# The last output DMA of a gated attention and GLU kernel in two parts, and one weight load in one piece

## The chip, the cores and the metric

The kernel runs on one core of a Trainium2 chip. The metric is device time in microseconds (us) of one execution; of several executions the median is given. A profile of one execution goes with it: its times are microseconds from the first instruction, and its span runs from the first to the last instruction. The engines are TensorE (PE; its weight loads are PEld), VectorE (DVE), ScalarE (ACT), GpSimd (POOL) and SyncE (SP). A `q` behind a name (SPq, ACTq) marks what the engine's sequencer does by itself: issuing DMAs, waiting for semaphores. Sixteen DMA engines move data between the chip's main memory and the core's own memory.

## The reference

One input `x` of 2048 rows and 512 columns (bf16) goes through a linear attention block and through a gated SwiGLU block, and a gate for each row mixes both:

```python
x = A_x
g = _sigmoid((x * gate_w).sum(-1, keepdims=True))
a = _A_ref(x, A_wqkv, A_wo)        # 32 heads of 16; phi(q), phi(k); kv and z summed over the rows
b = _B_ref(x, B_w1, B_w3, B_w2)    # (silu(x @ w1) * (x @ w3)) @ w2, 1376 hidden columns
return g * a + (1 - g) * b
```

The output has 2048 rows of 512 bf16 values, 2.10 MB in all.

## The kernel before, in words

All is unrolled into one straight program, and the order of every engine's instructions is the order in which the kernel's text gives them. Rows are taken in 16 tiles of 128 (`t`) or 4 blocks of 512 (`tb`).

- **Loads (lines 108 to 143).** Nearly all DMAs are issued by SP (`dq = nc.sync`), one after the other: the first rows `xN` (line 116), the projection weights `wqk` (113), 14 transposed loads of `x` into `xT` (110) with natural loads `xN` between them (128), the gate column and the remainder columns `wr` (130 to 134), then `w1` in one DMA and `w3` in two (the loop of lines 135 to 137), `wv` (138), `wo` (139) and `w2` (142, 143). ACT issues a single DMA, `touch` (line 120), 8 KB at the very start, whose data nothing reads.
- **Projections (lines 339 to 374).** `q` and `k` of each row tile by matmul (line 167), the function phi on ACT and DVE (lines 180 to 187), sums on POOL (199), and the products of `pk` and `xN` (line 215).
- **GLU (`glu_step`, lines 257 to 274).** For each of the 4 blocks and each of 10 column chunks of 128: four matmuls with `w1` (line 262), four with `w3` (line 268), silu on ACT, product on DVE into `hT`. The 96 remaining columns are done by `rem_step` (221 to 255). In the first block the small attention matrices (`kv_step` with `wv`, `m2_step` with `wo`) are made between the chunks.
- **Output (`out_step`, lines 408 to 444).** For each row tile: four matmuls give the attention part (line 414), ACT scales it by the gate into `aga` (419), eleven matmuls with `w2` give the GLU part (427), DVE combines both into `o` (431), and SP writes the rows of `o` to memory (444). For the last tile (`last`) the columns are computed in three strips, 256, 128 and 128 wide. The first strip is written by a DMA of its own; the second is not written by itself (lines 439 to 443), and the third one's DMA writes the last 256 columns, 128 rows of 512 B.

Each DMA carries a completion semaphore out of eight that are used in rotation over all DMAs of the program, SP's and ACT's together; a DMA from the ninth on first waits until the DMA eight places before it has landed. At the program's end SP waits for all completion semaphores, and a barrier over the five engines follows (its instructions bear the line of the launch, L493; L498 in the changed kernel, whose lines from 441 on stand five lower).

Of the kernel before, what the change touches and what calls it, by code (L numbers as in the profile page):

```python
# [16 lines left out]
def kernel(  # L17
# [17 lines left out]
    nc = tc.nc  # L35
    P = nc.NUM_PARTITIONS
# [5 lines left out]
    KC = D // P  # L42
# [15 lines left out]
    w1_r = B_w1.rearrange("(kc d) f -> d kc f", d=P)  # L58
    w3_r = B_w3.rearrange("(kc d) f -> d kc f", d=P)
# [16 lines left out]
        out=bmask[:], in_=bmask[:], pattern=[[-Dh, HPC], [0, Dh]], compare_op=ALU.is_ge,  # L76
# [3 lines left out]
        out=bmask[:], in_=bmask[:], pattern=[[Dh, HPC], [0, Dh]], compare_op=ALU.is_ge,  # L80
# [20 lines left out]
    w1 = consts.tile([P, KC, F0], BF16, name="w1")  # L101
    w3 = consts.tile([P, KC, F0], BF16, name="w3")
# [3 lines left out]
    dq = nc.sync  # L106
# [22 lines left out]
    with nc.allow_non_contiguous_dma(reason="gate column"):  # L129
        dq.dma_start(  # L130
            out=wr[:, :, 2 * FR : NR], in_=gate_w.rearrange("(kc d o) -> d kc o", d=P, o=1)
        )
    dq.dma_start(out=wr[:, :, 0:FR], in_=w1_r[:, :, F0:F])
    dq.dma_start(out=wr[:, :, FR : 2 * FR], in_=w3_r[:, :, F0:F])
    for w, w_r, cuts in ((w1, w1_r, (0, KC)), (w3, w3_r, (0, 2, KC))):
        for a, b in zip(cuts, cuts[1:]):
            dq.dma_start(out=w[:, a:b, :], in_=w_r[:, a:b, 0:F0])
    dq.dma_start(out=wv[:], in_=wqkv_r[:, :, 2 * D : 3 * D])
# [22 lines left out]
    def ab_tile():  # L161
        turn["ab"] += 1
        return bank[(turn["ab"] - 1) % 4]
# [244 lines left out]
    def out_step(tb, tt):  # L408
        t = tb * TPB + tt
        ts = slice(t * P, (t + 1) * P)  # L410
        tl = slice(tt * P, (tt + 1) * P)
        a_ps = ab_tile()
        for c in range(KC):
            nc.tensor.matmul(  # L414
                a_ps[:], lhsT=pqT[:, c, ts], rhs=M2[:, c, :],
                start=(c == 0), stop=(c == KC - 1),
            )
        aga = work.tile([P, D], FP32, tag="aga", name="aga")
        nc.scalar.activation(out=aga[:], in_=a_ps[:], func=ACT.Copy, scale=g_all[:, t : t + 1])  # L419
        o = work.tile([P, D], BF16, tag="o", bufs=3, name="o")  # L420
        last = t == NT - 1
        for lo, w in ((0, 2 * P), (2 * P, P), (3 * P, P)) if last else ((0, D),):
            cs = slice(lo, lo + w)
            b_ps = ab_tile()
            for fc in range(FC + 1):
                n = P if fc < FC else FR
                nc.tensor.matmul(  # L427
                    b_ps[:, 0:w], lhsT=hT[tb][:n, fc, tl], rhs=w2[:n, fc, cs],
                    start=(fc == 0), stop=(fc == FC),
                )  # L430
            nc.vector.scalar_tensor_tensor(  # L431
                out=o[:, cs], in0=b_ps[:, 0:w], scalar=omg_all[:, t : t + 1], in1=aga[:, cs],
                op0=ALU.mult, op1=ALU.add,
            )
            if t < 2:
                rows = out2d[0 : 2 * P, :].rearrange("(p j) d -> p j d", j=2)[:, t, :]
            else:
                rows = out2d[ts, :]
            if last and w == P:

                if lo + w < D:
                    continue
                cs = slice(2 * P, D)
            dq.dma_start(out=rows[:, cs], in_=o[:, cs])

    den_products(0)
    den_at = {0: 0, 1: 1, 3: 2, 6: 3}
    for tb in range(NTB):
        for fc in range(FC):
            glu_step(tb, fc)  # L450
            if tb == 0:
                if fc in den_at:
                    den_step(den_at[fc])
                if fc == 2:
                    kv_step()
                if fc == 4:
                    m2_step()
                if fc == 7:
                    rem_step(0)
        for tt in range(TPB):  # L460
            out_step(tb, tt)
            if tb + 1 < NTB:
                if tt == 0:
                    hT[tb + 1] = work.tile([P, FC + 1, TB], BF16, tag="hT", name="hT")
                if tt == 1:
                    rem_step(tb + 1)
                den_step((tb + 1) * TPB + tt)
# [30 lines left out]
```

## Time and profile before

| what | value |
|---|---|
| median of 3 runs | 179.43 us (179.19 to 179.78) |
| the profiled execution | 179.22 us |
| its span | 177.5 us |
| PE matmul busy | 173.9 us, 98% |
| DVE, ACT, POOL busy | 100.5, 62.3, 62.9 us |
| granted TensorE clock | 1.00 |
| bytes read and written in main memory | 8.43 and 2.10 MB |
| output DMAs | 15 of 128 KB (median 1.9 us to landing), 2 of 64 KB (1.5 us) |

The page's section 2 cuts the span into 40 slices of 4.4 us; each digit is the busy share of a slice in tenths. Section 4 follows the chain that ended last back from the last instruction. In rows of instructions, "x3: 351/351/484" is a count and the shortest, median and longest duration in ns; "DMA to landing" is counted from the start of the issue to the last of a DMA's completion marks. A DMA has up to 16 such marks, one from each DMA engine. The trace also holds a record of every DMA packet with its queue, start, duration and size.

### The profile page before, as it was taken

The page shows a single profiled execution, that of the slowest core. Times are in us where ns is not written, and L with a number is a line of the kernel's source. Part 1 is how long each engine was busy: PE and PEld are TensorE (multiplying, and loading weights), DVE is VectorE, ACT ScalarE, POOL GpSimd, SP SyncE. Part 2 cuts the span into 40 slices and gives each one's busy share as a digit, 9 for nine tenths or more (in the row PEclk, how much of TensorE's full clock was granted, in tenths as well). Part 3 has the DMA queues.
Part 4 walks back from the last instruction along what each step waited for, and adds up shares of the span by engine and source line. Part 5 has one row for each costly group of instructions (what it writes and reads, how often), then busy time and mean ns, then how long its engine had stood idle before and what let it go on. Part 6 is the DMA issues. An engine that isn't in the chain of part 4 may idle for free.

```text
span 177.5 us, 2504 instructions
## 1 busy us (share of the span) xinstructions
PE 173.9 (98%) x880; PEld 84.1 (47%) x880; DVE 100.5 (57%) x195; ACT 62.3 (35%) x113; POOL 62.9 (35%) x105
## 2 busy tenths in 40 slices
PE   8999999999999999999999999999999999999993
PEld 5444444444454464644444464444445444444453
DVE  1399788888899663575434166634325664433222
ACT  3354544444735441332342223142322223342130
POOL 5086656656577240446200044540004432000000
PEclk9999999999999999999999999999999999999999
DMA  5989869994002120233100013520000342000001
GB/s 174 269 202 216 163 106 264 406 381 142 4 0 59 30 47 16 59 82 96 30 0 4 0 40 80 90 63 0 0 0 30 89 92 59 0 0 0 30 33 59
DMA packets 28940, 15.15 MB, mean 85 GB/s; under 512 B 20896, under 2 KB 27264, under 8 KB 28928
## 3 DMA queue, kind: packets, MB, share of 16 engines
q1 hardware_dynamic: 28656, 14.98, 32.3%
q8 instruction: 7, 0.11, 0.3%
q14 instruction: 5, 0.04, 0.1%
q10 hardware_dynamic: 272, 0.01, 0.1%
HBM read 8.43 MB, written 2.10 MB: 59 GB/s over the span
## 4 chain that ended last, share of the span: by engine, by line
PE 98%; DVE 0%; issue 0%
PE bank L427 21%; PE bank L262 19%; PE bank L268 19%; PE bank L167 16%; PE bank L414 8%; PE bank L215 8%; PE bank L229 3%; PE bank L315 2%; PE bank L389 1%; PE bank L402 0%; PE bank L321 0%; DVE o L431 0%; PE bank L376 0%
## 5 line engine op out<-in xcount | busy, mean ns | idle before, releaser
L274 DVE TENSOR_TENSOR hT<-bank,sg 128x512 bf16<-128x512 f32 x40 | 27.2, 681 | 30.9 <-PE bank L268 30.9
L268 PE MATMUL bank<-xT,w 128*128 128x512 bf16 x160 | 41.1, 379 | 0.0
L262 PE MATMUL bank<-xT,w 128*128 128x512 bf16 x160 | 41.1, 379 | 0.0
L427 PE MATMUL bank<-w,hT 128*128 128x512 bf16 (+3 forms) x198 | 40.7, 355 | 0.0
L273 ACT ACTIVATE sg<-bank 128x512 bf16<-128x512 f32 x40 | 23.9, 597 | 46.9 <-PE bank L262 46.9
L296 POOL TENSOR_TENSOR pqs<-pq,rden 128x512 bf16<-128x512 bf16 x16 | 16.9, 1055 | 65.1 <-issue 60.0
L167 PE MATMUL bank<-wqk,xT 128*128 128x512 bf16 x128 | 30.6, 382 | 0.0
L431 DVE SCALAR_TENSOR_TENSOR o<-bank,omg_all,aga 128x512 bf16<-128x512 f32 (+2 forms) x18 | 12.5, 692 | 28.1 <-PE bank L427 28.0
L427 PEld LDWEIGHTS <-hT 128*128 128x128 bf16 (+1 forms) x198 | 18.5, 98 | 19.8
L199 POOL TENSOR_TENSOR zacc<-zacc,pk 128x128 f32<-128x128 f32 x56 | 23.3, 446 | 10.4 <-DVE pk L185 10.4
L268 PEld LDWEIGHTS <-w 128*128 128x128 bf16 x160 | 15.7, 98 | 18.9
L262 PEld LDWEIGHTS <-w 128*128 128x128 bf16 x160 | 15.6, 98 | 18.5
L419 ACT ACTIVATE aga<-bank,g_all 128x512 f32<-128x512 f32 x16 | 11.0, 687 | 28.9 <-PE bank L414 28.9
L167 PEld LDWEIGHTS <-xT 128*128 128x128 bf16 x128 | 12.5, 98 | 15.0 <-issue 0.5
L281 POOL TENSOR_TENSOR pr<-pq,zb 128x512 f32<-128x512 bf16 x16 | 18.4, 1153 | 1.7 <-DVE zb L377 1.7
L414 PE MATMUL bank<-M,pqT 128*128 128x512 bf16 x64 | 16.4, 378 | 0.0
L215 PE MATMUL bank<-pk,xN 128*128 128x512 bf16 x64 | 16.4, 379 | 0.0
L180 ACT ACTIVATE eq<-bank 128x512 bf16<-128x512 f32 x16 | 9.4, 597 | 16.0 <-PE bank L167 16.0
L185 DVE SCALAR_TENSOR_TENSOR pk<-bank,emk 128x512 bf16<-128x512 f32 x16 | 11.1, 692 | 1.6
L180 ACT ACTIVATE ek<-bank 128x512 bf16<-128x512 f32 x16 | 9.4, 597 | 6.6 <-PE bank L167 6.6
L185 DVE SCALAR_TENSOR_TENSOR pq<-bank,emq 128x512 bf16<-128x512 f32 x16 | 11.1, 692 | 0.6
L285 DVE TENSOR_REDUCE den<-pr 128x32 f32<-128x512 f32 x16 | 10.8, 676 | 0.0
(50 smaller groups left out, 81.7 us busy)
## 6 DMA issues: line engine op xcount, KB each, us to landing
w<-in_B_w_dram SPq DMA_DIRECT2D x4, 640.0 KB, 9.6
out_dram<-o SPq DMA_DIRECT2D x15, 128.0 KB, 1.9
xN<-in_A_x_dram SPq DMA_DIRECT2D x3, 512.0 KB, 4.5
w<-in_B_w_dram SPq DMA_DIRECT2D x1, 1280.0 KB, 7.6
wqk<-in_A_wqkv_dram SPq DMA_DIRECT2D x4, 256.0 KB, 3.7
xN<-in_A_x_dram SPq DMA_DIRECT2D x2, 256.0 KB, 2.9
wv<-in_A_wqkv_dram SPq DMA_DIRECT2D x1, 512.0 KB, 10.7
wo<-in_A_wo_dram SPq DMA_DIRECT2D x1, 512.0 KB, 11.1
```

The source lines that it names most:

```text
L167: nc.tensor.matmul(ps[:], lhsT=xT[:, kc, t * P : (t + 1) * P], rhs=w[:, kc, :], start=(kc == 0), stop=(kc == KC - 1),)
L180: nc.scalar.activation(out=e[:], in_=ps[:], func=ACT.Exp)
L185: nc.vector.scalar_tensor_tensor(out=dst, in0=ps[:], scalar=0.0, in1=em[:], op0=ALU.max, op1=ALU.add)
L199: nc.gpsimd.tensor_tensor(out=(zaccb if t == NT - 1 else zacc)[:, cs], in0=zacc[:, cs], in1=pk[t][:, cs], op=ALU.add,)
L215: nc.tensor.matmul(bank[kc][:], lhsT=xN[:, t, kc * P : (kc + 1) * P], rhs=pk[t][:], start=(t == 0), stop=(t == NT - 1),)
L262: nc.tensor.matmul(g_ps[:], lhsT=w1[:, kc, fs], rhs=xT[:, kc, tok], start=(kc == 0), stop=(kc == KC - 1),)
L268: nc.tensor.matmul(u_ps[:], lhsT=w3[:, kc, fs], rhs=xT[:, kc, tok], start=(kc == 0), stop=(kc == KC - 1),)
L273: nc.scalar.activation(out=sg[:], in_=g_ps[:], func=ACT.Silu)
L274: nc.vector.tensor_tensor(out=hT[tb][:, fc, :], in0=u_ps[:], in1=sg[:], op=ALU.mult)
L281: nc.gpsimd.tensor_tensor(out=pr[t][:], in0=pq[:, t, :], in1=zb[:], op=ALU.mult)
L414: nc.tensor.matmul(a_ps[:], lhsT=pqT[:, c, ts], rhs=M2[:, c, :], start=(c == 0), stop=(c == KC - 1),)
L427: nc.tensor.matmul(b_ps[:, 0:w], lhsT=hT[tb][:n, fc, tl], rhs=w2[:n, fc, cs], start=(fc == 0), stop=(fc == FC),)
```

## The change

Two edits. The third strip's DMA of the last tile, 128 rows, becomes two: rows 64 to 127 are issued by ACT, rows 0 to 63 by SP. And `w3` is loaded by one DMA, not by two.

```diff
-    for w, w_r, cuts in ((w1, w1_r, (0, KC)), (w3, w3_r, (0, 2, KC))):
+    for w, w_r, cuts in ((w1, w1_r, (0, KC)), (w3, w3_r, (0, KC))):
         for a, b in zip(cuts, cuts[1:]):
             dq.dma_start(out=w[:, a:b, :], in_=w_r[:, a:b, 0:F0])
...
                 if lo + w < D:
                     continue
                 cs = slice(2 * P, D)
+            if last and w == P:
+
+                nc.scalar.dma_start(out=rows[P // 2 : P, cs], in_=o[P // 2 : P, cs])
+                dq.dma_start(out=rows[0 : P // 2, cs], in_=o[0 : P // 2, cs])
+                continue
             dq.dma_start(out=rows[:, cs], in_=o[:, cs])
```

The number of DMAs stays the same, with one fewer on SP among the loads and one more, on ACT, at the end. In the rotation of completion semaphores every DMA from `wv` to the last tile's first strip stands one place earlier. All matmuls, and all instructions of DVE and POOL, keep their order; the waits of some for a DMA name another semaphore of the eight, and one weight load of line 268 loses its wait for the second half of `w3`.

## The prediction

> **What bounds the kernel now.** I read the page's busy times first, then the rows of the 40 slices.
>
> ```profile
> span 177.5 us, 2504 instructions
> PE 173.9 (98%) x880; PEld 84.1 (47%) x880; DVE 100.5 (57%) x195; ACT 62.3 (35%) x113; POOL 62.9 (35%) x105
> ...
> PE   8999999999999999999999999999999999999993
> ...
> PEclk9999999999999999999999999999999999999999
> DMA  5989869994002120233100013520000342000001
> ```
>
> TensorE is busy from slice 2 to slice 39 at the full clock; the 16 DMA engines are loaded only up to slice 10 (about 44 us). Only the last slice, 4.4 us long, has PE mostly idle, and that is where the first part of the change sits. Next, the chain that ended last, at its end:
>
> ```profile
> 169.90 1.51 PE bank L427 x7
> 171.41 0.87 PE bank L414 x4
> 172.28 2.46 PE bank L427 x33
> 174.73 0.03 issue
> 174.76 0.35 DVE o L431
> ```
>
> The last matmul ends at 174.73, the last combine (`o`, 128x128) at 175.11. The span ends at 177.5, so 2.39 us follow in which no compute engine works. What they hold is in the rows of the last line of `out_step` and of the program's end (launch line), and in the queue's own waits:
>
> ```profile
> L444 SPq DMA_DIRECT2D out_dram<-o x2: 332/332/332, 174.1 to 175.1; - x2
> ...
> DMA to landing us min/median/max: 1.5/1.5/1.5
> ```
>
> ```profile
> SPq L444 <- DVE o L431: 2.0, 2, 1.4
> SPq L493 <- DMA out_dram<-o: 0.9, 1, 0.9
> ```
>
> The first fence is asked of tile `o` from 173 to 178: two DMAs of 332 ns on SP, the second at 175.135, each landing 1.5 us after its issue. SP then waits 0.9 us for that landing. The rest is the end barrier. Four short windows show the same stretch from the DMA side (columns after the window: its length, then busy us and count of PE, PEld, DVE, ACT and POOL, clock, DMA share, GB/s):
>
> ```profile
> 175.10:175.90 0.80, 0.00 (x0) 0.00 (x0) 0.01 (x1) 0.00 (x0) 0.00 (x0) 1.00 0.09 26
> 175.90:176.40 0.50, 0.00 (x0) 0.00 (x0) 0.00 (x0) 0.00 (x0) 0.00 (x0) 1.00 0.44 131
> 176.40:176.70 0.30, 0.00 (x0) 0.00 (x0) 0.00 (x0) 0.00 (x0) 0.00 (x0) 1.00 0.00 0
> 176.70:177.50 0.80, 0.00 (x0) 0.00 (x0) 0.00 (x0) 0.00 (x0) 0.00 (x0) 1.00 0.00 0
> ```
>
> The bytes of the last DMA move only in the second window (what moves in the first is the tail of the DMA before). The packet records behind it: first packet at 175.970, last at 176.315; 128 packets of 512 B, eight on each DMA engine at 26 ns, so 0.21 us an engine, and the engines start some 0.16 us apart. The 16 landing marks come from 176.499 to 176.664. So the 2.39 us are: 0.03 to the issue, 0.84 from issue to first packet, 0.35 of packets, 0.35 from the last packet to the last mark, 0.84 of barrier. **A split can touch only the 0.35 us of packets and, by little, the issue.**
>
> **Part one, the last output DMA as two.** It removes one DMA of 128 rows x 512 B on SP and adds two of 64 rows x 512 B, ACT's first in the program, then SP's. Both wait for the same combine, which ends at 175.11, and for a completion semaphore last used long ago (the program has eight in rotation; the two earlier users were issued at 142.6 and 144.4). Behind ACT's instruction stands only its part of the end barrier, behind SP's only the waits of the end; nobody else waits for either.
>
> - Issue: 332 ns for 128 rows of 512 B and 332 for most of 1 KB. For 64 rows no row exists. SP's longer shapes, 512 rows in 505 to 580 ns, give (505-332)/384 = 0.45 ns a row, so 64 rows less save at most 0.03 us. I take 0.
> - Packets: the same 128 packets on the same 16 engines, whether from one queue or two. If only one half existed, each engine would have 4 instead of 8: 4 x 26 = 0.10 us less. The 128 KB rows show the size of this term: alone on the engines they land in 1.70 us against 1.53 for 64 KB, 0.17 for doubled bytes. Bounds: -0.10 (the halves do not disturb each other at all) to +0.16 (the engines are started twice, 0.16 us each time). I take 0, because both halves use the same engines together.
> - The end's waits: SP goes through the semaphores in pairs, at 175.514, 175.583, 175.649, 175.714 and, after the wait, 176.680, 0.065 us a step. ACT's DMA takes the place of the second last output in the rotation (SP's becomes the last), and the former last semaphore is checked one step after it. If SP is held at ACT's semaphore, one more step of 0.065 us follows the landing; if SP's half lands later, none. I take +0.05.
> - ACT as issuer: ACT has been idle since 173.0 (its last `aga` ran 172.31 to 173.00), so it can be at the wait in time. The single DMA it has issued is `touch` at the start:
>
> ```profile
> L120 ACTq DMA_DIRECT2D touch<-in_A_wqkv_dram x1: 434/434/434, 0.9 to 0.9; - x1
> ...
> DMA to landing us min/median/max: 2.9/2.9/2.9
> ```
>
> It took 434 ns to issue (256 pieces of 32 B; SP's of two pieces a row take 468 to 582) and landed in 2.9 us, where SP's 1 KB gate column took 2.8 and the first `xN` 2.7. That speaks for an issuer as quick as SP. Against it: its first packet came 1.92 us after issue, `xN`'s 1.04 us. But in that time the engines carried `xN`'s packets (1.8 to 2.3 us), so part of it is queueing. Bounds for ACT's lateness: 0 to 1.92-1.04 = 0.88 us. I take 0, nearer to the two durations that have a like partner; 0.88 is a rival.
>
> Can the two issues proceed together? `touch` ran 0.85 to 1.29 while SP's first `xN` issue ran 0.80 to 1.19, and it was not longer than SP's alone. So I add nothing; the other end is one full issue, +0.33 us.
>
> The Trainium skill ("DMA: Bandwidth & Descriptors", Rules for kernel authors) says of two transfers to the two partition halves: don't bother, they share the same 16 engines; that agrees with the zero for the packets, and by it alone nothing would be won. "Perfetto Trace Analysis" (DMA Instruction — HWDGE) goes further: the descriptor generator is shared and locked for one sequencer at a time, so the second half would start an issue later. The overlap of `touch` and `xN` above does not show such a lock; by the rule the sum would be that of the second rival below instead of the forecast.
>
> **Part two, w3 in one DMA.** It removes one SP issue (468 ns plus a gap of about 0.05, so 0.51 us); `wv`, `wo` and `w2` are issued up to 0.51 us earlier, every later DMA moves by one place in the rotation of completion semaphores, and one DMA wait of PE on L268 goes. Bytes and row pieces are the same (2,560 B). The cover: the halves of w3 landed at 35.5 and 35.1 us and their first use is the weight load of L268 at 47.1, so 11.6 us of slack; `w1` 33.9 for 46.3; `wv` 38.6 for 51.4; `wo` 40.0 for 55.8; the last `w2` 43.6 for 67.5. From 43.7 to 52.0 PE is busy the whole 8.30 us. So the gain and the cost are both 0. Were the cover gone, PE would stall by the full lateness, which would need a landing 11.6 us later than now. The shifted rotation makes a DMA wait for the one eight places before it; all of these landed before their successors came up (`wr`, `w1`, `w3` at 28 to 36 us for the first `pqT` at 52.1), so nothing is late next.
>
> **Sum.** The profiled execution took 179.22 us (span 177.5 and 1.72 around it). 0 - 0 + 0 + 0.05 = +0.05, so 179.27 against its own time. The median of the three runs is 179.43, 0.21 above that execution: 179.48, rounded to **179.5**.
>
> **Rivals.**
>
> - **Slower: ACT's queue starts late.** Place: between ACT's issue at 175.14 and its first packet. Price: 0.88 us later, less 0.10 for the smaller half that then runs alone, plus the step of 0.065: +0.85, 180.3 us (+0.5%). It decides over 0.3% (0.54 us, about what a measurement of this kernel can tell from no change) from 0.58 us of lateness on. For it: 1.92 against 1.04 us; the queue will have rested 170 us. Against: `touch` landed only 0.15 us slower than `xN`, and the engines were occupied meanwhile. Chance 0.15.
> - **One issue after the other.** The second half starts 0.33 us later, runs alone (-0.10), and the extra step of 0.065 counts: +0.30, 179.73. Still within 0.3%. Chance 0.17.
> - **It pays a little.** Both halves take -0.10 in packets and -0.03 in issue, and no step is added: -0.13, 179.3. The 0.17 us between 64 and 128 KB speaks for it, that the engines are shared speaks against. Chance 0.10. A gain beyond 0.54 us would need more than all 0.35 us of packets; 0.03 is left for what I do not see.
> - **w3 late** needs a landing 11.6 us later; it is among the 0.02 that I take from the other cases for slower.
>
> **Numbers.** Forecast 0.55. The runs of before spread from 179.19 to 179.78; with the forecast's -0.10 to +0.16 that is 179.1 to 179.94, and with the second rival's +0.30 on the highest run 180.1. So the range is **179.1 to 180.1**; it leaves out most of the late ACT queue. Slower by over 0.3%: 0.15 + 0.02 of the others; faster: 0.03; within: 0.80.
>
> **What would show it.** PE's last matmul again at 174.7 and the last combine ending at 175.1: then part two is nothing. ACT's DMA issued at 175.14 with SP's, both about 0.33 us or less; ACT's landing 1.4 to 1.6 us later: forecast. About 1.8: one after the other. Over 2.1: late queue. The span's end 0.84 to 0.90 us after the last landing: the barrier. I am wrong if PE's end moves, since then something in the loads or in the order of PE that I costed at nothing carries a price, or if the landing falls below 1.4 us.

## The result and the profile after

The changed kernel is slower: 180.36 us (median of 18 runs, 179.47 to 180.88) against 179.63 for the kernel before (18 runs, 179.12 to 180.07; the three runs shown earlier had 179.43). The ratio is 1.0037, 95% interval 1.0023 to 1.0050, so about 0.66 us, with 0.41 to 0.90 as the interval. The profiled execution took 180.39 us with a span of 178.6.

The page of the kernel after, the same lines as shown of before:

```profile
span 178.6 us, 2489 instructions
PE 172.8 (97%) x864; PEld 83.9 (47%) x880; DVE 100.4 (56%) x195; ACT 62.2 (35%) x113; POOL 62.9 (35%) x105
...
PE   7899999999999999999999999999999999999992
...
PEclk9999999999999999999999999999999999999999
DMA  5978949993002120233100013510001342000011
```

PE's middle is unchanged. Differences stand at both ends: a little less PE in the first two slices, and a longer stretch without PE in the last. The sixteen matmuls fewer are records missing from this trace; their weight loads are all there. Next, the rows of tile `o` from 173 us on (duration min/median/max in ns, then first and last start):

```profile
L449 SPq DMA_DIRECT2D out_dram<-o x2: 332/332/333, 172.7 to 174.5; - x2
L447 SPq DMA_DIRECT2D out_dram<-o x1: 559/559/559, 175.6 to 175.6; - x1
L446 ACTq DMA_DIRECT2D out_dram<-o x1: 557/557/557, 175.6 to 175.6; - x1
...
DMA to landing us min/median/max: 1.5/1.8/2.1
```

Here the loss shows at once. The two outputs of 128 rows just before (line 449) are issued in 332 and 333 ns, the two halves in 559 and 557; SP's half landed 1.85 us after its issue and ACT's 2.12, where the whole DMA of before landed after 1.53. SP's own wait for the last landing grew from 0.9 to 1.4 us:

```profile
SPq L498 <- DMA out_dram<-o: 1.4, 1, 1.4
```

Four windows over the end, from the last combine on (the columns as before; the DMA share is the last but one):

```profile
175.54:176.70 1.16, 0.00 (x0) 0.00 (x0) 0.00 (x0) 0.00 (x0) 0.00 (x0) 1.00 0.06 16
176.70:177.40 0.70, 0.00 (x0) 0.00 (x0) 0.00 (x0) 0.00 (x0) 0.00 (x0) 1.00 0.37 94
177.40:177.70 0.30, 0.00 (x0) 0.00 (x0) 0.00 (x0) 0.00 (x0) 0.00 (x0) 1.00 0.00 0
177.70:178.60 0.90, 0.00 (x0) 0.00 (x0) 0.00 (x0) 0.00 (x0) 0.00 (x0) 0.68 0.02 9
```

(The clock of 0.68 stands behind PE's last instruction and costs nothing.) Before, the last bytes began to move 0.86 us after the combine and took 0.35; now 1.23 us pass first and then 0.58. I call **tail** the time from the end of the last combine to the end of the span: 2.39 us before, 3.05 after, so +0.66. That is the size of the measured loss. It splits into +0.60 until the last landing (1.56 to 2.16) and +0.06 in the barrier (0.84 to 0.90).

The spans differ by more, 1.09 us. The rest, 0.43, is already there when PE ends (174.72 against 175.15), and it was made in the first 12 us, as PE's waits from 0 to 15 us show:

```profile
PE bank L167 <- DMA wqk<-in_A_wqkv_dram: 0.7, 2, 0.4
```

In the profile of before no such wait stands there. I take it for scatter and no part of the change: the loads up to `wr` are the same in both kernels, and in the profiles of the experiments below whose loads begin alike PE ended anywhere from 174.41 to 175.58. So the tail is read from the profiles, one of each kernel, and the times serve as a check. Where two runs share a piece of the tail it agrees to some hundredths: a whole DMA of 128 rows x 512 B, issued by SP at the end, landed 1.53 to 1.56 us after its issue in all three runs that have one last.

### The profile page after: what moved, and what is told of

Its sections match the earlier page's. It is cut to its first block, busy times and chain, and to the rows that moved or that the text cites. A ratio compares the mean times of both kernels' runs of the same rounds, so it can differ in the third digit from the quotient of the medians.

```text
span 178.6 us, 2489 instructions
## 1 busy us (share of the span) xinstructions
PE 172.8 (97%) x864; PEld 83.9 (47%) x880; DVE 100.4 (56%) x195; ACT 62.2 (35%) x113; POOL 62.9 (35%) x105
## 4 chain that ended last, share of the span: by engine, by line
PE 94%; DMA 2%; issue 1%; SPq 0%; DVE 0%
PE bank L427 21%; PE bank L262 20%; PE bank L268 19%; PE bank L167 15%; PE bank L215 8%; PE bank L414 8%; PE bank L229 3%; DMA wqk<-in_A_wqkv_dram 2%; PE bank L389 1%; PE bank L402 0%; SPq L113 0%; SPq L116 0%; DVE o L431 0%; PE bank L376 0%
## 5 line engine op out<-in xcount | busy, mean ns | idle before, releaser
L262 PE MATMUL bank<-xT,w 128*128 128x512 bf16 x158 | 41.0, 379 | 0.3
L427 PE MATMUL bank<-w,hT 128*128 128x512 bf16 (+4 forms) x197 | 40.6, 355 | 0.1
L268 PE MATMUL bank<-xT,w 128*128 128x512 bf16 x154 | 40.3, 379 | 0.2
```

Source lines behind the costliest of these rows:

```text
L262: nc.tensor.matmul(g_ps[:], lhsT=w1[:, kc, fs], rhs=xT[:, kc, tok], start=(kc == 0), stop=(kc == KC - 1),)
L268: nc.tensor.matmul(u_ps[:], lhsT=w3[:, kc, fs], rhs=xT[:, kc, tok], start=(kc == 0), stop=(kc == KC - 1),)
L427: nc.tensor.matmul(b_ps[:, 0:w], lhsT=hT[tb][:n, fc, tl], rhs=w2[:n, fc, cs], start=(fc == 0), stop=(fc == FC),)
```

## The experiments

Three theories for the +0.66. **T1**: two sequencers that issue at once hinder each other. **T2**: a DMA of 64 rows costs more than one of 128 by itself. **T3**: ACT's queue starts late (the prediction's first rival).

**The split alone** (the changed kernel with w3 again in two):

```diff
-    for w, w_r, cuts in ((w1, w1_r, (0, KC)), (w3, w3_r, (0, KC))):
+    for w, w_r, cuts in ((w1, w1_r, (0, KC)), (w3, w3_r, (0, 2, KC))):
```

> The split of the last output DMA alone, w3 again in two. Measured from the end of the last combine to the end of the span (2.39 us before, 3.05 after). All three theories lay the loss on the split, so all expect the tail at 3.0 us and the time 0.6 to 0.7 us above the kernel before. If instead w3 carries part of it, the time stands less than 0.4 us above.

Measured: ratio to before 1.0042 (1.0024 to 1.0060), tail 2.99 us, issues 559 and 556 ns, landings 1.86 and 2.13. The loss is the split's. The 0.06 less than in the changed kernel is the step of SP's waits: here ACT's semaphore is checked last, in the changed kernel one more follows.

**w3 alone** (before, with w3 in one DMA):

```diff
-    for w, w_r, cuts in ((w1, w1_r, (0, KC)), (w3, w3_r, (0, 2, KC))):
+    for w, w_r, cuts in ((w1, w1_r, (0, KC)), (w3, w3_r, (0, KC))):
```

> w3 in one DMA, the last output as before. Theory: no effect in the loads, the last DMA stands one place earlier in the rotation, so SP does one more step of 0.065 us after the landing: tail 2.45 us, time within 0.1 us of before beyond scatter. If the rival that w3 moves the loads were right, PE's last matmul would end later by several tenths in the median of the runs.

Measured: ratio 0.9994 (0.9976 to 1.0012), tail 2.46 us, landing 1.53 as before. w3 shows no effect in the loads, to within the interval's 0.2%; the one step at the end is there.

**Both halves on SP** (the changed kernel, ACT's half issued by SP):

```diff
-                nc.scalar.dma_start(out=rows[P // 2 : P, cs], in_=o[P // 2 : P, cs])
+                dq.dma_start(out=rows[P // 2 : P, cs], in_=o[P // 2 : P, cs])
```

> Both halves on SP, one after the other; ACT issues nothing at the end. Theory 1 (two sequencers issuing at once hinder each other): each issue back at about 0.33 us, first packet 0.84 us after the first issue, the second half 0.38 us behind the first: last landing 1.8 us after the first issue, tail 2.7 us. Theory 2 (a DMA of 64 rows costs more than one of 128 by itself): both issues stay at 0.56 us, last landing 2.4 us, tail 3.3 us. Theory 3 (ACT's queue starts late by itself): as theory 1, tail 2.7.

The row of line 446, the first of the two halves, when no other sequencer issues anything:

```profile
L446 SPq DMA_DIRECT2D out_dram<-o x1: 562/562/562, 175.9 to 175.9; - x1
...
DMA to landing us min/median/max: 1.9/1.9/1.9
```

562 ns and 1.86 us, and the second half 578 ns and 1.88 us. Tail 3.37, ratio 1.0054 (1.0033 to 1.0075). T1 falls: with one issuer the long issue stays. T2 gave 3.3.

**The whole DMA on ACT** (128 rows, ACT the only issuer at the end):

```diff
-                nc.scalar.dma_start(out=rows[P // 2 : P, cs], in_=o[P // 2 : P, cs])
-                dq.dma_start(out=rows[0 : P // 2, cs], in_=o[0 : P // 2, cs])
+                nc.scalar.dma_start(out=rows[:, cs], in_=o[:, cs])
```

> The last DMA whole, 128 rows, but issued by ACT. Theory 1: ACT alone is as quick as SP alone, issue 0.33 us, first packet 0.84, landing 1.53 us, plus 0.065 for the step: tail 2.45 us. Theory 2: the same 2.45. Theory 3: first packet at 1.4 us or later, landing 2.1, tail 3.0 us.

Measured: issue 361 ns, first packet 0.87 us after it, landing 1.56, tail 2.48; ratio 1.0024 (1.0003 to 1.0044), which the 0.09 us of the tail (0.05%) fit at the interval's lower end. T3 falls: ACT is 0.03 us slower than SP.

**Other row counts** (before; five outputs that stand alone are cut in two on SP):

```diff
+            cut = {4: 96, 8: 80, 12: 64, 13: 48, 14: 16}.get(t)
+            if cut:
+                dq.dma_start(out=rows[0:cut, cs], in_=o[0:cut, cs])
+                dq.dma_start(out=rows[cut:P, cs], in_=o[cut:P, cs])
+                continue
             dq.dma_start(out=rows[:, cs], in_=o[:, cs])
```

> Five output DMAs that stand alone on the engines (tiles 4, 8, 12, 13, 14, rows of 1 KB) are cut in two on SP; the first of each pair has 96, 80, 64, 48 and 16 rows. Whole, they issue in 0.33 us and land in 1.70. A (64 is a case of its own): only tile 12's first part takes 0.5 us or more to issue and over 1.15 us to its first packet; 96, 80, 48 and 16 rows issue in 0.33 to 0.36 and have their first packet at 0.85. B (every count but 128 and 32 is slow): four or five of the first parts take over 0.5 us. The time is not read, since ten DMAs stand for five.

SP's instructions of tiles 12, 13 and 14 in order of time (start and duration in us; line 446 is the first part, 447 the second):

```profile
165.49 0.56 SPq L446 DMA_DIRECT2D out_dram<-o  x1
166.10 0.58 SPq L447 DMA_DIRECT2D out_dram<-o  x1
168.74 0.34 SPq L446 DMA_DIRECT2D out_dram<-o  x1
169.13 0.41 SPq L447 DMA_DIRECT2D out_dram<-o  x1
171.98 0.32 SPq L446 DMA_DIRECT2D out_dram<-o  x1
172.34 0.41 SPq L447 DMA_DIRECT2D out_dram<-o  x1
```

Only the pair of 64 rows takes 0.56 and 0.58; 48 and 80 rows, 16 and 112 take 0.32 to 0.41. The first parts of 96, 80, 64, 48 and 16 rows had their first packet 0.84, 0.84, **1.21**, 0.84 and 0.82 us after issue. Here the rows are 1 KB long, in the changed kernel 512 B: 64 is slow in both. The expectation's case A came true.

**A quarter** (only rows 0 to 31, on SP):

```diff
-                nc.scalar.dma_start(out=rows[P // 2 : P, cs], in_=o[P // 2 : P, cs])
-                dq.dma_start(out=rows[0 : P // 2, cs], in_=o[0 : P // 2, cs])
+                dq.dma_start(out=rows[0 : P // 4, cs], in_=o[0 : P // 4, cs])
```

> One DMA of the last tile's rows 0 to 31, 512 B each, on SP; rows 32 to 127 of the last 256 columns are not written. A (a DMA of fewer than 128 rows takes a longer form of issue, whatever their number): issue 0.5 to 0.6 us, first packet 1.15 to 1.25 us after issue, landing 1.75 to 1.85, tail 2.75. B (the cost grows with the rows and 64 is a special case): issue 0.45 us or less, landing below 1.6.

Measured: issue 335 ns, first packet 0.84, landing 1.41, tail 2.34. B: few rows are not slow as such.

**ACT's half alone** (rows 64 to 127; SP's half left out):

```diff
-                dq.dma_start(out=rows[0 : P // 2, cs], in_=o[0 : P // 2, cs])
```

> Only ACT's half, rows 64 to 127; rows 0 to 63 of the last 256 columns are not written. A (the 64-row form is slow on each queue, and ACT's half came later in the changed kernel because it stood behind SP's half): landing 1.86 to 1.90 us after issue, as SP's first half in the run with both on SP, tail 2.8. B (ACT's half is late by itself): landing 2.1 us as in the changed kernel, tail 3.0.

The row of its last DMA:

```profile
L446 ACTq DMA_DIRECT2D out_dram<-o x1: 529/529/529, 175.2 to 175.2; - x1
```

Its first packet came 1.18 us after the issue's start, its landing 1.83; the tail is 2.77. A: ACT's half is as slow as SP's, not slower. In the changed kernel it landed 0.28 us after SP's because it stood behind it. The packet records say the same: SP's ran from 176.765, the last starting at 177.038, and ACT's first at 177.036.

**At once, with full rows** (128 rows each, cut by columns at 448, so that both wait for the third strip):

```diff
-                nc.scalar.dma_start(out=rows[P // 2 : P, cs], in_=o[P // 2 : P, cs])
-                dq.dma_start(out=rows[0 : P // 2, cs], in_=o[0 : P // 2, cs])
+                nc.scalar.dma_start(out=rows[:, 448:D], in_=o[:, 448:D])
+                dq.dma_start(out=rows[:, 2 * P : 448], in_=o[:, 2 * P : 448])
```

> Both last DMAs of 128 rows, issued at the same moment after the third strip: SP 192 columns (384 B a row), ACT 64 columns (128 B a row). A (only the 64-row form was slow, and a second queue costs its turn behind the first): SP's landing 1.5 us after issue; ACT's 0.2 to 0.35 us later; both issues below 0.45 us except for a wait of one for the other; tail 2.6 to 2.75 us. B (no turn: the 0.28 us between the halves of the changed kernel belong to the 64-row form too): both land within 0.1 us of 1.5 us, tail 2.4 to 2.45. C (two issues at once are slow in any form): issues 0.5 us or more, landings 1.8 and 2.1.

Measured: issues 333 ns (SP, at 175.994) and 374 (ACT, at 175.999), landings 1.52 and 1.68, tail 2.62; ratio 1.0016 (0.9998 to 1.0034). Between A and B: there is a turn (the second queue's DMA lands later than the first's), but of 0.16 us. C falls.

**The cut at row 48** (SP 48 rows, ACT 80, at once), which takes away the row count and leaves the rest of the change:

```diff
-                nc.scalar.dma_start(out=rows[P // 2 : P, cs], in_=o[P // 2 : P, cs])
-                dq.dma_start(out=rows[0 : P // 2, cs], in_=o[0 : P // 2, cs])
+                nc.scalar.dma_start(out=rows[48:P, cs], in_=o[48:P, cs])
+                dq.dma_start(out=rows[0:48, cs], in_=o[0:48, cs])
```

> The changed kernel with the cut at row 48 in place of 64: SP writes rows 0 to 47, ACT rows 48 to 127, both at once. A (the loss is mostly the 64-row form: 0.33 us of late first packet and issue, and the rest the turn of the second queue): both issues 0.33 to 0.45 us, SP's first packet 0.84 us after issue and landing 1.45 to 1.55, ACT's 0.15 to 0.25 later, tail 2.55 to 2.65 us against 3.05 in the changed kernel, time 0.2 us above before. B (any cut by rows over two queues is as slow): landings 1.8 and 2.1, tail 3.0, time 0.6 above.

The rows of tile `o` in this run:

```profile
L447 SPq DMA_DIRECT2D out_dram<-o x1: 336/336/336, 175.3 to 175.3; - x1
L446 ACTq DMA_DIRECT2D out_dram<-o x1: 379/379/379, 175.3 to 175.3; - x1
...
DMA to landing us min/median/max: 1.5/1.5/1.7
```

Tail 2.60 us, so 0.45 of the 0.66 is gone with the number 64. Ratio 1.0007 (0.9994 to 1.0020), all of it below the changed kernel's 1.0023 to 1.0050. What is left, 0.21, is 0.14 for the later landing of ACT's part and 0.07 for the barrier.

**Column halves**, 128 rows of 256 B each:

```diff
-                nc.scalar.dma_start(out=rows[P // 2 : P, cs], in_=o[P // 2 : P, cs])
-                dq.dma_start(out=rows[0 : P // 2, cs], in_=o[0 : P // 2, cs])
+                nc.scalar.dma_start(out=rows[:, 3 * P : D], in_=o[:, 3 * P : D])
+                dq.dma_start(out=rows[:, 2 * P : 3 * P], in_=o[:, 2 * P : 3 * P])
```

> The two halves by columns, not by rows: 128 rows of 256 B on SP and 128 rows of 256 B on ACT, issued at the same moment. A (the short row count is what is slow; two queues at once cost only their turn): issues 0.33 to 0.40 us, SP's first packet 0.84 us after issue, the later landing 1.6 to 1.85 us, tail 2.5 to 2.75, time 0.1 to 0.4 us above before. B (two issues at once hinder each other as well): issues 0.5 us or more, later landing 2.1, tail 3.0.

The expectation asked the wrong question: SP's half holds the second strip alone, so it was issued at 174.36, when that strip was ready, and ACT's at 174.99. They did not meet. Issues 378 and 360 ns, ACT's landing 1.48, tail 2.34, ratio 0.9997 (0.9983 to 1.0011). That is 0.05 us less tail than before and the best of the versions that write the whole output, but not to be told from before by its times. It is faster than the changed kernel by what that lost.

**Strips apart**, the same with the queues exchanged (second strip on ACT, third on SP):

```diff
-            if last and w == P:
-
-                if lo + w < D:
-                    continue
-                cs = slice(2 * P, D)
...
+            if last and lo == 2 * P:
+                nc.scalar.dma_start(out=rows[:, cs], in_=o[:, cs])
+                continue
```

> Each strip of the last tile written as soon as it is combined: the first, 256 columns, on SP, the second, 128 columns, on ACT, the third, 128 columns, on SP; all of 128 rows. The last DMA then carries 32 KB, not 64. A: full issue of 0.33 us, no neighbour at the same moment, landing 1.45 us or a little less, no extra step at the end: tail 2.3 us, 0.05 to 0.1 below before, which the times cannot tell from no change. B (rows of 256 B cost more than they save): landing 1.55 or more, tail 2.4 to 2.5.

Measured: ratio 1.0048 (1.0029 to 1.0067), tail 3.12, the third strip's landing 2.25 us after issue. Neither case; my expectation missed. The windows over that DMA (DMA share and GB/s at the end of each line):

```profile
175.85:176.15 0.30, 0.00 (x0) 0.00 (x0) 0.00 (x0) 0.00 (x0) 0.00 (x0) 1.00 0.58 130
176.15:176.50 0.35, 0.00 (x0) 0.00 (x0) 0.00 (x0) 0.00 (x0) 0.00 (x0) 1.00 0.00 0
176.50:176.65 0.15, 0.00 (x0) 0.00 (x0) 0.00 (x0) 0.00 (x0) 0.00 (x0) 1.00 0.06 14
```

Most packets move in the first window, then nothing moves for 0.35 us, then eight more follow. Fifteen of the 16 marks came by 176.465, the last at 177.276. In the packet records one packet of 8 KB, on the queue that brings instruction code, starts at 175.984 and takes 544 ns. The eight late packets, one engine's share, start at 176.524. They explain some 0.5 us of the late landing; the last mark came another 0.3 us late (0.64 us after that engine's last packet, 0.35 from the last packet of the others to their last mark), and that stays open. The 32 KB of this DMA, as many bytes as a half in the changed kernel but in 128 rows, were issued in 332 ns with the first packet after 0.83: the number of bytes is not what made the halves slow.

**Strips apart without `touch`**, to shift that packet by making ACT's program one instruction shorter:

```diff
-    touch = consts.tile([P, 2, 16], BF16, name="touch")
-    nc.scalar.dma_start(out=touch[:], in_=wqkv_r[:, 1:3, 0:16])
```

> The run with each strip written by itself, and without the load that ACT issues at the start, so that ACT's program is one instruction shorter. In that run an 8 KB packet of instruction code went over one DMA engine at 175.98 us for 544 ns, and that engine's eight output packets came 0.5 us after the others. A (the packet follows ACT's 191st recorded instruction by 1.2 to 1.3 us): it now falls after the last landing, which is back at 1.45 to 1.5 us after issue, and the tail is 2.30 to 2.36 us instead of 3.12. B (the packet comes at its own time, or the late engine has another cause): a landing of 1.9 us or more again, tail 2.7 or more.

Measured: the code packet came at 179.25, after everything; the third strip landed in 1.45 us with all 16 marks together. So A for the landing. The tail, 2.56, missed its 2.30 to 2.36, because ACT's step in the end barrier came 0.37 us after its release (0.09 in the other runs), and because the last DMA's semaphore was no longer the last checked (one step of 0.06). What held ACT there was not followed. The ratio, 1.0030 (1.0016 to 1.0045), also holds whatever `touch` does at the start, which was not followed either.

## Why the prediction was wrong, step by step

- **What bounds the kernel, and part two (w3).** Right: no gain and no cost that the times show (w3 alone: 0.9994, 0.9976 to 1.0012), only the one step of the final waits. One reading was off: w3's second half landed at 37.2 us, not at 35.1, which leaves about 10 us before its use, not 11.6; the conclusion stands.
- **Issue of 64 rows, "I take 0". This step failed.** I read a slope of 0.45 ns a row from longer shapes and bounded the issue only from below zero (at most -0.03). Measured: 559 ns for 332, and a first packet at 1.20 us for 0.84. SP's half landed 0.32 us later than the whole DMA, where I had allowed a gain of up to 0.10. So the sentence that a split can touch only the packets and, by little, the issue was wrong as well: it moved the stretch from issue to first packet, which I held fixed. Of 16, 32, 48, 64, 80, 96 and 128 rows, only 64 does this where no transpose was issued just before. No row of before had that count, and a slope carried below the shortest shape it came from was no bound. The rows of before also warned that an issue is not set by the row count alone:

```profile
L444 SPq DMA_DIRECT2D out_dram<-o x17: 332/376/602, 71.1 to 175.1; - x17
```

I had read 332 for most of the outputs of 1 KB rows. Of these 15, six took 332 to 337 ns and one 376, but eight took 529 to 602, each issued 0.09 to 0.13 us after a DMA transpose of the same queue. No transpose stands near the last DMA, so this is not its cause.

- **Can the two issues proceed together, "I add nothing".** This zero failed too, as did the zero for the packets: the second queue's landing comes 0.14 to 0.16 us after that of a single whole DMA (cuts at row 48 and at column 448), and in the changed kernel 0.28 after SP's half, where the packets of both halves ran one behind the other, 0.58 us for 0.35. The second rival, one issue after the other at +0.30, was nearest to what a cut without the slow form costs (+0.21).
- **The end's waits, +0.05.** Right: +0.06. The run with other row counts bears the step out: its last DMA, whole as in before, stands three places earlier in the rotation, and from its landing to the end of the span 1.04 us passed for 0.84.
- **ACT's queue late, the first rival.** Its price (+0.85) brought it near the measured time, and the sign I had set for it, a landing over 2.1 us, came true with 2.12. But it is not the cause: alone, ACT lands a whole DMA in 1.56 us and a half in 1.83, as SP does. A late landing named the place, not the reason.
- **The sum with measured sizes**: 0.32 (64-row form) + 0.28 (ACT's half behind it) + 0.06 (step) = 0.66, against +0.05 predicted.
- **The time.** Of the 0.86 us between 179.5 and 180.36, 0.2 is the median of before, 179.43 in three runs and 179.63 in eighteen.

The Trainium skill's rule in "DMA: Bandwidth & Descriptors" (Rules for kernel authors), not to split a transfer over the partition halves, is borne out; its reason, that the two serialize, fits the halves, whose packets ran one behind the other, and not the cut at row 48, where they overlapped. It puts no price on the split: here the halves lost 0.66 us of tail, and the better of the two cuts by rows over two queues 0.21. Its rule in "Perfetto Trace Analysis" (DMA Instruction — HWDGE), that one sequencer at a time holds the descriptor generator, fits one row of the changed kernel: ACT's packets begin as SP's end. It does not fit the issues: begun 5 ns apart, they took 559 and 557 ns, where alone SP's took 562 and ACT's 529, so neither waited for the other by an issue's length. Nor does it fit the cut at row 48, where both issues ran together (336 and 379 ns) and ACT's packets began at 176.261 while SP's still started until 176.485. The measurement decides: with the quick form a second issue cost about 0.15 us, not a whole issue.

That the loss comes from the row count of 64 is shown; why 64 rows are slow stays open. It holds for rows 0 to 63 and 64 to 127, for 512 B and 1 KB, on SP and (rows 64 to 127 of 512 B) on ACT. Other directions of transfer, 112 rows alone and counts that are no multiple of 16 were not tried.

## What to carry to other kernels

Before a DMA's shape is changed, look for a row of exactly the new shape, or measure it alone: here issue and first packet were not a smooth function of the row count. At the end of this kernel the last DMA is mostly latency outside its packets (1.18 of its 1.53 us stand before the first packet and after the last), so halving its bytes cannot win much, while a second queue adds its turn and a step of the final waits. Writing what is ready earlier by itself, in full rows, took 0.05 us off the tail in one run, which its times could not tell from none; the same cut with the queues exchanged was slower by 0.48%.

## What the runs showed of the hardware

- A DMA of 64 rows to main memory was issued in 529 to 578 ns, with its first packet 1.18 to 1.21 us after the issue's start when no other output stood before it. With other counts from 16 to 128 rows it was 315 to 382 ns and 0.82 to 0.89 us (0.92 and 0.98 for ACT's DMA issued at once with SP's), and 412 to 418 ns for the second of a pair on SP.
- An output DMA of 128 rows issued right behind a DMA transpose of the same queue took 512 to 678 ns to issue (all 123 such rows of the 14 profiles; eight of the kernel before).
- Instruction code travels over the same DMA engines, as far as one run shows: in all 14 profiles the last 8 KB packet of code started 1.0 to 1.9 us after ACT's 191st recorded instruction, and in strips apart, where it met an output DMA, one engine's share of that DMA came late and the landing grew from 1.45 to 2.25 us. Eight of the profiles have two instructions more on ACT near the end than before; in this one the packet fell among the output's packets, in the other seven behind them. That the count of ACT's instructions sets it is an inference from these 14 traces and the one run in which the packet moved.
